# Zero matmuls in TensorE's first gaps, longer planned DMA times, and another order of the first loads in a planned attention-and-mixer kernel

## The chip, the cores and the metric

The kernel runs on one core of a Trainium2 chip. A core has five engines with queues of their own, each working strictly in the order of its queue: TensorE (PE in the profile, its weight loads PEld), VectorE (DVE), ScalarE (ACT), GpSimd (POOL) and SyncE (SP), and DMA engines that all queues share. Loads that change the type from fp32 to fp16 are issued by POOL; transposes by DMA and the stores are issued by SP. The metric is the device time of one execution in microseconds (us), and less is better. Times are medians of several executions; the profile is of one execution.

## The reference

Two stages follow each other. The first is sigmoid attention over 8 batches, 12 heads, 448 positions and 64 values a head; the second is a mixer over the result laid out as 448 x 768:

```
scores = q @ k.T / sqrt(64) - log(448)
attn   = sigmoid(scores) @ v                 # per batch and head
x      = attn laid out as (8, 448, 768)
h      = relu(x.T @ w_tok1) @ w_tok2         # w_tok1 448 x 256, w_tok2 256 x 448
u      = x + h.T
out    = u + relu(u @ w_ch1) @ w_ch2         # w_ch1 768 x 1536, w_ch2 1536 x 768
```

Inputs and output are fp32. The kernel computes in fp16 with fp32 accumulation.

## The kernel before

A batch's attention is cut into three units of four heads, (batch, unit). For each unit k, q and v are loaded, k and q are turned (the 64 head values brought onto the partitions), and seven rounds follow: matmuls of a round's scores (`score`, L499), the sigmoid on ACT (`sig`, L514). After them the value matmuls (`values`, L536) collect the unit's output in PSUM, a copy brings it to SBUF as `xT` (`take`, L567 or L569), and it is turned back into `x`. From a whole `x` follow the token mixing (K1, L721, then relu, then K2, L751, added to x as `u`), a cast and a turn of `u` to `uT`, and the channel mixing: C1 (L828, twelve blocks of six matmuls, relu on DVE) and C2 (L873, and L882 for the tail rows of two batches together).

Batches 0 and 1 are turned by TensorE (`tk` and `tq`, L456, copied from PSUM by DVE at L469). From batch 2 on POOL permutes k and q (`permute`, L433) and SP turns them by DMA (kT, qT, L438); SP also turns `xT` to `x` (L578) and `u` to `uT` (L808), and stores the output. Batch 0's chain is finer: its token mixing runs by unit (K1 at L621, relu, then KT at L650, which adds the second product onto the unit's values in PSUM, and the copy to `uT`, L665 on ACT or L667 on DVE).

Nothing of the order is left to the hardware: every step is an `Op` with an engine, an estimated time, the steps that it follows and the buffers that it uses, and `Plan.run` lays all of them out by a list schedule with these estimates. The outcome is a fixed instruction order for each engine. Where a real time is longer than the estimate, the engine waits at that place and everything behind it waits too. Four estimates matter here. `lag` is what lies between the end of a step and the start of one on another engine. A load's time is a pipe that all loads share (`pipe`), with at most eight DMAs of POOL outstanding (`landed`). A DMA transpose of SP ends at `far`, 3.0 us, after its start, and up to 5 us later while loads are planned to be under way. `choose` picks TensorE's next step by readiness and priority: steps in `extra` by their own `pri` (0 to 2.5 for the turns and batch 0's chain), attention groups by due times, then K, C1 and C2.

Before any data is there, `run_up` (L411) lets TensorE multiply zeros nine times, into a PSUM bank called `idle`. That is one of four banks which the turns, the units' values, K and C all share; `idle` goes back once its users have ended. Loads of POOL come in a written order; from unit 6 on, each load also waits for a sigmoid of the unit three places before it (the `mark` copies, L685).

One thing in the code acts otherwise than it reads: the closures `keep`, `relu` and `lay` of batch 0 read `last` when they are emitted, and by then it holds the value of the last unit. The copy of the second half of `uT` therefore runs on ACT (L665) for all three units, while the plan counts it on DVE for the first two.

Of the kernel before, what the change touches and what calls it, by code (L numbers as in the profile page):

```python
# [55 lines left out]
class Plan:  # L56
# [4 lines left out]
    def __init__(self, pools):  # L61
        self.pools, self.slots, self.ops = pools, {}, []
        self.log, self.kept = [], {}
        self.far = 3.0
        self.landed, self.pipe = [0.0] * 8, 0.0

    def buf(self, *a, **k):
# [2 lines left out]
    def op(self, name, engine, us, emit, after=(), uses=(), rank=0.0):  # L70
        o = Op(name, engine, us, emit, after, uses, rank)
        self.ops.append(o)
        return o

    def lag(self, d, o):
        return 0.0 if d.engine == o.engine == "PE" else self.LAG[d.engine]

    def slot_time(self, held, o):
# [39 lines left out]
    def run(self, choose):  # L118

        lists = {}  # L120
        for o in self.ops:
            if o.engine != "PE":
                lists.setdefault(o.engine, []).append(o)
        free = dict.fromkeys([*lists, "PE", "POOL"], 0.0)
        free["POOL"] = 1.3
        mode = [None]
        left = len(self.ops)
        while left:
            best = None
            for e, ops in lists.items():  # L130
                if e == "LD":
                    ops = ops[:1]
                for o in ops:
                    r = self.ready(o)
                    if r is None:
                        continue
                    at = free[e]
                    if e == "LD":
                        at = max(free["POOL"], self.landed[-8])
                    key = (max(r, at), o.rank, r)  # L140
                    if best is None or key < best[0]:
                        best = (key, e, o)
            pick = choose(self, free["PE"])
            if pick is not None:
                t, ops, kind = pick
                if best is None or t <= best[0][0]:
                    for o in ops:
                        r = self.ready(o)
                        t = max(t, r, free["PE"])
                        if kind != mode[0]:  # L150
                            t += 0.1
                            mode[0] = kind
                        self.hold(o)
                        o.start, o.end = t, t + o.us
                        free["PE"] = t = o.end
                        self.log.append(o)
                        left -= 1
                    continue
            if best is None:
                raise RuntimeError(  # L160
                    "\n".join(
                        f"{o.name} <- {[d.name for d in o.after if d.end is None]}"
                        for o in self.ops
                        if o.start is None
                    )[:6000]
                )
            (t, _, _), e, o = best
            self.hold(o)
            o.start = t
            if e == "LD":  # L170
                free["POOL"] = t + o.n * o.issue
                slow = 1.0 if self.pipe > 8.0 else 1.5
                self.pipe = max(self.pipe, free["POOL"] + 1.5) + slow * o.us
                o.end = self.pipe
                self.landed += [o.end] * o.n
            elif e == "SP":
                free[e] = t + o.us
                o.end = t + self.far + min(5.0, max(0.0, self.pipe - t - 0.5))
            else:
                o.end = free[e] = t + o.us  # L180
            lists[e].remove(o)
            self.log.append(o)
            left -= 1
        self.log.sort(key=lambda o: o.start)
        for o in self.log:
            o.emit()
# [3 lines left out]
def kernel(  # L190
# [12 lines left out]
    nc = tc.nc  # L203
# [7 lines left out]
    NQ = H // 4  # L211
    NDB = D // 128
    NCB = CC // 128
    DH = D // 2
    att_scale = 1.0 / math.sqrt(E)
    att_bias = -math.log(S)
    LEAD, SPAN, REST, WIDE = 12.0, 0.86, 1.0, 2

    assert (B, H, S, E) == (8, 12, 448, 64) and D == 768 and TT == 256 and CC == 1536

# [2 lines left out]
    plan = Plan({"sbuf": pa, "psum": pp})  # L223
# [31 lines left out]
    def mm(n):  # L255
        return n / 2400 + 0.003
# [50 lines left out]
        yield op(f"ld_{what}_{b}_{m}", "LD", 1.12, emit, uses=[t])  # L307

    def load_all(b, m):
        parts = {what: load_qkv(b, m, what) for what in ("k", "q", "v")}  # L310
        if (b, m) == (0, 0):
            for _ in range(2):
                for what in ("k", "q"):
                    o = next(parts[what])
                    loads[(b, m, what)][0].append(o)
        for what, ops in parts.items():
            made = list(ops)
            loads[(b, m, what)][0].extend(made)

    def load_w_tok():  # L320
        view = moe_w_tok1.rearrange("(p j) t -> p j t", j=J)

        def emit():
            nc.gpsimd.dma_start(out=w_tok1[0:64, :, :], in_=view)
            for slot, j0, n in ((0, 4, 3), (3, 3, 1), (4, 0, 3)):
                nc.gpsimd.dma_start(
                    out=w_tok1[64:128, slot : slot + n, :], in_=view[:, j0 : j0 + n, :]
                )

        a = op("ld_tok1", "LD", 2.3, emit, uses=[w_tok1])  # L330
        a.n, a.issue = 4, 0.54

        def emit2():
            nc.gpsimd.dma_start(
                out=w_tok2_s[:, :, :],
                in_=moe_w_tok2.rearrange("(tc t) s -> t tc s", tc=2),
            )
# [3 lines left out]
        for a_, z, j, n in ((0, 6, 0, 3), (1, 6, 4, 3), (6, 8, 3, 1), (8, 14, 4, 3), (9, 14, 0, 3)):  # L341
# [7 lines left out]
            spreads.append(  # L349
                op(f"spread{a_}", "DVE", 0.45, spread, [b], [w_tok2_s, w_tok2], rank=-1 if a_ < 7 else 2)  # L350
            )
        return a, spreads

    def load_ch1(i):
        def emit():
# [17 lines left out]

        return op(f"ld_ch2_{i}", "LD", 3.9, emit, uses=[w_ch2[i]])

    load_all(0, 0)
    load_all(0, 1)
    tok1_ld, tok2_ld = load_w_tok()
    load_all(0, 2)
    ch1_ld, ch2_ld = [], []  # L380
    load_all(1, 0)
    ch1_ld.append(load_ch1(0))
# [32 lines left out]
    up = op("up", "PE", 3.4, run_up, [blank_op], [idle, uT[0]])  # L415
    up.pri = -2
    extra.append(up)

    def turned(b, m, what, side):

# [22 lines left out]
            return [op(f"turn{what}_{b}_{m}", "SP", 1.3, turn, [o], [t, pm], rank=0)] * 2, t  # L443
        parts = [range(2)] if (b, m) != (0, 0) else [range(1), range(1, 2)]
        done = []
        hold = uT_ops[0][-2:] if (b, m) == (1, 2) else []
        for hs in parts:
            ps = bank(f"t{what}_{b}_{m}_{hs[0]}", [128, J, 2, P], FP16)
            r = slice(64 * hs[0], 64 * hs[-1] + 64)
# [26 lines left out]
    def attention(b):  # L476
# [4 lines left out]
        for m in range(NQ):  # L481
# [164 lines left out]
            for s in range(2):  # L646
# [14 lines left out]
                extra.append(o)  # L661

                def keep(s=s, m=m, ps=pa_):
                    if s == 1 and last:
                        nc.scalar.activation(out=uT[0][:, 2 * m + s, :], in_=ps[s](every), func=COPYF)  # L665
                    else:
                        nc.vector.tensor_copy(out=uT[0][:, 2 * m + s, :], in_=ps[s](every))  # L667

                uT_ops[0].append(
                    op(f"uT_{b}_{m}_{s}", "ACT" if s == 1 and last else "DVE", 0.6, keep, [o], [ps[s], uT[0]], rank=-2.5)  # L670
                )
        return rounds

# [23 lines left out]
    def token(b):  # L697
# [12 lines left out]
        else:  # L710
# [3 lines left out]
            for n, c in enumerate(cuts):  # L714
                need = [x_ops[(b, m)][-1 if b < 2 else n] for m in range(NQ)]
                for t in range(2):
# [9 lines left out]
                                stop=(blk == 3),  # L726
                            )

                    o = op(f"K1_{b}_{n}_{t}", "PE", 4 * mm(DH), tok1, [*need, tok1_ld], [ps, X[b], w_tok1, h1[b]])
                    first.append(o)  # L730

                    def relu(ps=ps, c=c, t=t):
# [243 lines left out]
    def choose(plan, t):  # L976
# [14 lines left out]
        for rank, kinds in ((2, K), (3, C1), (4, C2)):  # L991
            n = 0
            for row in kinds:
# [12 lines left out]
                        break  # L1006
                if n > (3 if rank == 2 else 0):
                    break
        if not cands:
            return None  # L1010
        first = min(c[0] for c in cands)
# [37 lines left out]
```

## Time and profile before

| what | value |
|---|---|
| median of 3 runs | 404.08 us (403.29 to 408.87) |
| the profiled execution's own time | 407.89 us |
| its span, first to last instruction | 406.1 us |
| PE busy in it | 375.8 us (93%) |
| ACT, DVE, POOL busy | 206.3, 160.7, 116.2 us |
| mean granted TensorE clock | 0.967 |

The profile shows one execution. Rows of a timeline give the start and duration of a run of instructions in us, the engine, the line of the kernel, the output and input tiles and shapes, how many, and in brackets how long the engine had been idle and what released it. Rows of a table by stretches give, for a window from A to B, its length, then the busy time of PE, PEld, DVE, ACT and POOL, the granted clock (1.00 is full speed, 0.50 half) and what DMA moved. Of a line's rows, the three numbers after a count are the smallest, median and largest duration in ns, and the last two the first and last start. Names such as `x<-xT` say which tile is written from which. SPq is SP's queue, which issues the transposes.

### The profile page before, as it was taken

The page shows a single profiled execution, that of the slowest core. Times are in us where ns is not written, and L with a number is a line of the kernel's source. Part 1 is how long each engine was busy: PE and PEld are TensorE (multiplying, and loading weights), DVE is VectorE, ACT ScalarE, POOL GpSimd, SP SyncE. Part 2 cuts the span into 40 slices and gives each one's busy share as a digit, 9 for nine tenths or more (in the row PEclk, how much of TensorE's full clock was granted, in tenths as well). Part 3 has the DMA queues.
Part 4 walks back from the last instruction along what each step waited for, and adds up shares of the span by engine and source line. Part 5 has one row for each costly group of instructions (what it writes and reads, how often), then busy time and mean ns, then how long its engine had stood idle before and what let it go on. Part 6 is the DMA issues. An engine that isn't in the chain of part 4 may idle for free.

```text
span 406.1 us, 7874 instructions
## 1 busy us (share of the span) xinstructions
PE 375.8 (93%) x3213; PEld 193.2 (48%) x3213; DVE 160.7 (40%) x295; ACT 206.3 (51%) x253; POOL 116.2 (29%) x264
## 2 busy tenths in 40 slices
PE   7889999999979996798999995799999999999995
PEld 3446545545434542354445552344445556555563
DVE  3155545265333422352341341363342245754231
ACT  3686666568746754285646754287564460300000
POOL 9773136333334433224341423223300000000000
PEclk9599999999999999799999999699999999999998
DMA  6999999969996999399958999599902454500343
GB/s 83 171 172 205 209 199 144 151 93 169 118 136 111 183 201 124 50 141 158 147 84 149 159 172 167 78 154 151 135 2 65 105 117 95 109 0 2 77 97 98
DMA packets 98724, 50.56 MB, mean 124 GB/s; under 512 B 72320, under 2 KB 95040, under 8 KB 98688
## 3 DMA queue, kind: packets, MB, share of 16 engines
q0 software_dynamic: 24320, 21.93, 40.9%
q1 hardware_dynamic: 74368, 28.13, 38.2%
q8 instruction: 25, 0.41, 0.4%
q14 instruction: 11, 0.09, 0.1%
HBM read 43.84 MB, written 11.01 MB: 135 GB/s over the span
## 4 chain that ended last, share of the span: by engine, by line
PE 82%; DMA 8%; ACT 5%; POOL 2%; DVE 1%; issue 1%; SPq 0%; POOLq 0%; ACTq 0%
PE c L828 26%; PE c L873 22%; PE qk L499 10%; PE xa L536 8%; PE yn L751 5%; DMA x<-xT 5%; PE k L721 5%; ACT attn L514 3%; PE c L882 3%; DMA uT<-u 2%; DMA k<-in_k_dram 1%; PE tq L456 1%; PE tk L456 1%; ACT u L780 1%; POOL k L291 1%
## 5 line engine op out<-in xcount | busy, mean ns | idle before, releaser
L514 ACT ACTIVATE attn<-qk,att_bias 128x896 f16<-128x896 f32 (+1 forms) x172 | 161.2, 989 | 101.3 <-PE qk L499 101.0
L828 PE MATMUL c<-uT,w_ch 128*128 128x448 f16 x576 | 117.8, 353 | 3.4 <-DMA uT<-u 3.2
L873 PE MATMUL c<-w_ch,h2aT 128*128 128x384 f16 x576 | 98.8, 326 | 0.0
L853 DVE TENSOR_SCALAR h2aT<-c 128x448 f16<-128x448 f32 x96 | 60.0, 625 | 83.1 <-PE c L828 82.9
L828 PEld LDWEIGHTS <-w_ch 128*128 128x128 f16 x576 | 53.2, 98 | 60.9 <-issue 15.9
L873 PEld LDWEIGHTS <-h2aT 128*128 128x128 f16 x576 | 55.1, 98 | 40.6 <-issue 5.1
L897 DVE TENSOR_TENSOR u<-u,c 128x384 f32<-128x384 f32 x48 | 26.6, 554 | 77.2 <-PE c L873 77.2
L499 PE MATMUL qk<-qT,kT 64*64 64x448 f16 x672 | 53.2, 370 | 1.4 <-ACT attn L514 0.9
L536 PE MATMUL xa<-attn,v 64*64 64x448 f16 x672 | 38.2, 360 | 0.5 <-ACT attn L514 0.5
L721 PE MATMUL k<-x,w_tok 128*128 128x384 f16 x112 | 23.0, 361 | 14.9 <-DMA x<-xT 14.9
L685 POOL COPY mark<-attn 1x1 f16<-1x1 f16 x54 | 9.6, 178 | 88.5 <-ACT attn L514 88.5
L433 POOL COPY kp<-k 128x384 f16<-128x384 f16 (+1 forms) x54 | 21.3, 428 | 45.2 <-DMA k<-in_k_dram 45.2
L569 ACT ACTIVATE xT<-xa 128x448 f16<-128x448 f32 x43 | 21.1, 545 | 19.1 <-PE xa L536 18.0
L499 PEld LDWEIGHTS <-kT 64*64 64x64 f16 x672 | 15.2, 107 | 30.6 <-issue 27.5
L772 DVE TENSOR_TENSOR u<-x,yn 128x384 f32<-128x384 f16 x48 | 24.4, 549 | 10.2 <-PE yn L751 10.1
L433 POOL COPY qp<-q 128x384 f16<-128x384 f16 (+1 forms) x54 | 21.3, 432 | 20.0 <-DMA q<-in_q_dram 14.3
L536 PEld LDWEIGHTS <-v 64*64 64x64 f16 x672 | 19.9, 109 | 14.7 <-issue 3.0
L751 PE MATMUL yn<-h,w_tok 128*128 128x384 f16 x128 | 26.3, 328 | 0.0
L733 DVE TENSOR_SCALAR h<-k 128x384 f16<-128x384 f32 x28 | 15.6, 558 | 25.0 <-PE k L721 23.5
L780 ACT ACTIVATE u<-u 128x768 f16<-128x768 f32 x21 | 17.5, 846 | 15.3 <-DVE u L772 15.3
L721 PEld LDWEIGHTS <-w_tok 128*128 128x128 f16 x112 | 11.2, 106 | 26.6 <-DMA x<-xT 11.2
L751 PEld LDWEIGHTS <-w_tok 128*128 128x128 f16 x128 | 10.9, 98 | 12.5 <-issue 6.4
(56 smaller groups left out, 189.3 us busy)
## 6 DMA issues: line engine op xcount, KB each, us to landing
out_dram<-u SPq DMA_DIRECT2D x48, 192.0 KB, 2.9
k<-in_k_dram POOLq DMA_DIRECT2D x21, 224.0 KB, 5.3
q<-in_q_dram POOLq DMA_DIRECT2D x21, 224.0 KB, 4.8
v<-in_v_dram POOLq DMA_DIRECT2D x21, 224.0 KB, 5.2
w_ch<-in_moe_w_ch_dram POOLq DMA_DIRECT2D x6, 768.0 KB, 16.0
out_dram<-ut SPq DMA_DIRECT2D x8, 192.0 KB, 3.1
v<-in_v_dram POOLq DMA_DIRECT2D x6, 112.0 KB, 4.8
x<-xT SPq DMA_TRANSPOSE x36, 4.4
```

The source lines that it names most:

```text
L433: nc.gpsimd.tensor_copy(out=pm[:, to, :, :], in_=src[:, fr, :, :])
L499: nc.tensor.matmul(out=ps[64 * s : 64 * s + 64, h, 0:S], lhsT=kT[64 * h : 64 * h + 64, i, s, :], rhs=qT[64 * h : 64 * h + 64, :, s, :], st ...
L514: nc.scalar.activation(out=at[:, hs, :], in_=ps[:, hs, 0:S], func=SIGMOID, bias=bias_t[:, :], scale=att_scale,)
L536: nc.tensor.matmul(out=ps[s](slice(64 * h, 64 * h + 64)), lhsT=vf[64 * s : 64 * s + 64, h, order[i], :], rhs=attn[i][64 * s : 64 * s + 64, ...
L721: nc.tensor.matmul(out=ps[:, :], lhsT=w_tok1[:, w1_slot(side, blk), 128 * t : 128 * t + 128], rhs=X[b][:, x_block(side, blk), c], start=(b ...
L751: nc.tensor.matmul(out=ps[:, :], lhsT=w_tok2[:, t, s0 : s0 + 2, :], rhs=h1[b][:, t, c], start=(t == 0), stop=(t == 1),)
L772: nc.vector.tensor_tensor(out=to, in0=x, in1=y, op=ADD)
L780: nc.scalar.activation(out=u16[rows, :], in_=utile[rows, :] if blk == 3 else u[b][:, blk, :], func=COPYF)
L828: nc.tensor.matmul(out=to(), lhsT=w_ch1[cb // 4][:, db, 128 * (cb % 4) : 128 * (cb % 4) + 128], rhs=uT[b][:, db, :], start=(db == 0), stop ...
L853: nc.vector.tensor_scalar(out=h2aT[b][:, cb, :], in0=to(), scalar1=0.0, scalar2=None, op0=MAX)
L873: nc.tensor.matmul(out=ps[:, :], lhsT=h2aT[b][:, cb, 128 * blk : 128 * blk + 128], rhs=w, start=(cb == 0), stop=(cb == NCB - 1),)
L897: nc.vector.tensor_tensor(out=t, in0=t, in1=ps[:, :], op=ADD)
```

## The change

Five things differ.

1. Planned times: `far` goes from 3.0 to 4.5 us; a load counts as landed 2.0 us later than the pipe says once the pipe is past 50 us (`load_far`); and 2.0 us instead of 0.12 us are planned between a step of POOL and the step of SP that follows it (`sp_wait`), which are the permutes and the turns of batches 2 to 7.
2. Fillers: while the plan's time is between 4 and 21 us (`FILL`), and no step of TensorE is ready within 0.2 us, the plan puts in one matmul of zeros, 128x128 by 256 columns, counted at 0.11 us. They write the bank `idle`; one last filler, made ahead, is put in at 21 us, and until then the bank is not given back.
3. The first loads: k and q of unit (0,0), k and q of (0,1), v of (0,0), a first part of w_tok1 (three DMAs, what batch 0 needs), w_tok2, k and q of (0,2), v of (0,1), v of (0,2), and the rest of w_tok1 (two DMAs; K1 of odd batches follows it). Before, k, q and v of (0,0) and of (0,1) came first, then all of w_tok1 (four DMAs), w_tok2, then k, q and v of (0,2).
4. The turns of unit (1,1) are held until batch 0's last `uT` copies are done, as those of (1,2) were already.
5. The second half of `uT` is copied by DVE for unit (0,0), and by ACT for (0,1) and (0,2), in the plan and in what is emitted.

```diff
--- before.py
+++ after.py
@@ -61,7 +61,7 @@
     def __init__(self, pools):
         self.pools, self.slots, self.ops = pools, {}, []
         self.log, self.kept = [], {}
-        self.far = 3.0
+        self.far, self.load_far, self.sp_wait = 4.5, 2.0, 2.0
         self.landed, self.pipe = [0.0] * 8, 0.0
 
     def buf(self, *a, **k):
@@ -73,6 +73,8 @@
         return o
 
     def lag(self, d, o):
+        if d.engine == "POOL" and o.engine == "SP":
+            return self.sp_wait
         return 0.0 if d.engine == o.engine == "PE" else self.LAG[d.engine]
 
     def slot_time(self, held, o):
@@ -124,8 +126,8 @@
         free = dict.fromkeys([*lists, "PE", "POOL"], 0.0)
         free["POOL"] = 1.3
         mode = [None]
-        left = len(self.ops)
-        while left:
+        self.left = len(self.ops)
+        while self.left:
             best = None
             for e, ops in lists.items():
                 if e == "LD":
@@ -154,7 +156,7 @@
                         o.start, o.end = t, t + o.us
                         free["PE"] = t = o.end
                         self.log.append(o)
-                        left -= 1
+                        self.left -= 1
                     continue
             if best is None:
                 raise RuntimeError(
@@ -168,10 +170,11 @@
             self.hold(o)
             o.start = t
             if e == "LD":
+                far = self.load_far if self.pipe > 50.0 else 0.0
                 free["POOL"] = t + o.n * o.issue
                 slow = 1.0 if self.pipe > 8.0 else 1.5
                 self.pipe = max(self.pipe, free["POOL"] + 1.5) + slow * o.us
-                o.end = self.pipe
+                o.end = self.pipe + far
                 self.landed += [o.end] * o.n
             elif e == "SP":
                 free[e] = t + o.us
@@ -180,7 +183,7 @@
                 o.end = free[e] = t + o.us
             lists[e].remove(o)
             self.log.append(o)
-            left -= 1
+            self.left -= 1
         self.log.sort(key=lambda o: o.start)
         for o in self.log:
             o.emit()
@@ -215,6 +218,7 @@
     att_scale = 1.0 / math.sqrt(E)
     att_bias = -math.log(S)
     LEAD, SPAN, REST, WIDE = 12.0, 0.86, 1.0, 2
+    FILL = 21.0
 
     assert (B, H, S, E) == (8, 12, 448, 64) and D == 768 and TT == 256 and CC == 1536
 
@@ -307,29 +311,29 @@
         yield op(f"ld_{what}_{b}_{m}", "LD", 1.12, emit, uses=[t])
 
     def load_all(b, m):
-        parts = {what: load_qkv(b, m, what) for what in ("k", "q", "v")}
-        if (b, m) == (0, 0):
-            for _ in range(2):
-                for what in ("k", "q"):
-                    o = next(parts[what])
-                    loads[(b, m, what)][0].append(o)
-        for what, ops in parts.items():
-            made = list(ops)
+        for what in ("k", "q", "v"):
+            made = list(load_qkv(b, m, what))
             loads[(b, m, what)][0].extend(made)
 
-    def load_w_tok():
+    def load_w_tok1(part):
+
         view = moe_w_tok1.rearrange("(p j) t -> p j t", j=J)
+        moves = (
+            ((0, 0, 0, 4), (64, 0, 4, 3), (64, 3, 3, 1)),
+            ((0, 4, 4, 3), (64, 4, 0, 3)),
+        )[part]
 
         def emit():
-            nc.gpsimd.dma_start(out=w_tok1[0:64, :, :], in_=view)
-            for slot, j0, n in ((0, 4, 3), (3, 3, 1), (4, 0, 3)):
+            for r, slot, j0, n in moves:
                 nc.gpsimd.dma_start(
-                    out=w_tok1[64:128, slot : slot + n, :], in_=view[:, j0 : j0 + n, :]
+                    out=w_tok1[r : r + 64, slot : slot + n, :], in_=view[:, j0 : j0 + n, :]
                 )
 
-        a = op("ld_tok1", "LD", 2.3, emit, uses=[w_tok1])
-        a.n, a.issue = 4, 0.54
-
+        a = op(f"ld_tok1_{part}", "LD", 1.3 if part == 0 else 1.0, emit, uses=[w_tok1])
+        a.n, a.issue = len(moves), 0.58
+        return a
+
+    def load_w_tok2():
         def emit2():
             nc.gpsimd.dma_start(
                 out=w_tok2_s[:, :, :],
@@ -349,7 +353,7 @@
             spreads.append(
                 op(f"spread{a_}", "DVE", 0.45, spread, [b], [w_tok2_s, w_tok2], rank=-1 if a_ < 7 else 2)
             )
-        return a, spreads
+        return spreads
 
     def load_ch1(i):
         def emit():
@@ -373,10 +377,25 @@
 
         return op(f"ld_ch2_{i}", "LD", 3.9, emit, uses=[w_ch2[i]])
 
-    load_all(0, 0)
-    load_all(0, 1)
-    tok1_ld, tok2_ld = load_w_tok()
-    load_all(0, 2)
+    early = {(m, what): load_qkv(0, m, what) for m in range(NQ) for what in ("k", "q", "v")}
+
+    def load_early(m, *what):
+        for _ in range(2):
+            for x in what:
+                for o in early[(m, x)]:
+                    loads[(0, m, x)][0].append(o)
+                    if m == 0 and x != "v":
+                        break
+
+    load_early(0, "k", "q")
+    load_early(1, "k", "q")
+    load_early(0, "v")
+    tok1_ld = load_w_tok1(0)
+    tok2_ld = load_w_tok2()
+    load_early(2, "k", "q")
+    load_early(1, "v")
+    load_early(2, "v")
+    tok1_late = load_w_tok1(1)
     ch1_ld, ch2_ld = [], []
     load_all(1, 0)
     ch1_ld.append(load_ch1(0))
@@ -415,6 +434,20 @@
     up = op("up", "PE", 3.4, run_up, [blank_op], [idle, uT[0]])
     up.pri = -2
     extra.append(up)
+    fill = {"n": 0}
+
+    def filler():
+
+
+        def emit():
+            nc.tensor.matmul(
+                out=idle[:, 0:256], lhsT=uT[0][:, 0, 0:128], rhs=uT[0][:, 0, 0:256], start=True, stop=True
+            )
+
+        fill["n"] += 1
+        return op(f"fill_{fill['n']}", "PE", 0.11, emit, [up], [idle])
+
+    fill["last"] = filler()
 
     def turned(b, m, what, side):
 
@@ -443,7 +476,7 @@
             return [op(f"turn{what}_{b}_{m}", "SP", 1.3, turn, [o], [t, pm], rank=0)] * 2, t
         parts = [range(2)] if (b, m) != (0, 0) else [range(1), range(1, 2)]
         done = []
-        hold = uT_ops[0][-2:] if (b, m) == (1, 2) else []
+        hold = uT_ops[0][-2:] if b == 1 and m else []
         for hs in parts:
             ps = bank(f"t{what}_{b}_{m}_{hs[0]}", [128, J, 2, P], FP16)
             r = slice(64 * hs[0], 64 * hs[-1] + 64)
@@ -661,13 +694,13 @@
                 extra.append(o)
 
                 def keep(s=s, m=m, ps=pa_):
-                    if s == 1 and last:
+                    if s == 1 and m:
                         nc.scalar.activation(out=uT[0][:, 2 * m + s, :], in_=ps[s](every), func=COPYF)
                     else:
                         nc.vector.tensor_copy(out=uT[0][:, 2 * m + s, :], in_=ps[s](every))
 
                 uT_ops[0].append(
-                    op(f"uT_{b}_{m}_{s}", "ACT" if s == 1 and last else "DVE", 0.6, keep, [o], [ps[s], uT[0]], rank=-2.5)
+                    op(f"uT_{b}_{m}_{s}", "ACT" if s == 1 and m else "DVE", 0.6, keep, [o], [ps[s], uT[0]], rank=-2.5)
                 )
         return rounds
 
@@ -726,7 +759,7 @@
                                 stop=(blk == 3),
                             )
 
-                    o = op(f"K1_{b}_{n}_{t}", "PE", 4 * mm(DH), tok1, [*need, tok1_ld], [ps, X[b], w_tok1, h1[b]])
+                    o = op(f"K1_{b}_{n}_{t}", "PE", 4 * mm(DH), tok1, [*need, tok1_ld, *([tok1_late] if side else [])], [ps, X[b], w_tok1, h1[b]])
                     first.append(o)
 
                     def relu(ps=ps, c=c, t=t):
@@ -1006,6 +1039,22 @@
                         break
                 if n > (3 if rank == 2 else 0):
                     break
+        if t >= FILL and fill["last"]:
+            extra.append(fill["last"])
+            fill["last"] = None
+        if 4.0 < t < FILL and (not cands or min(c[0] for c in cands) > t + 0.2) and up.start is not None:
+            o = fill.get("op")
+            if o is None or o.start is not None:
+                o = fill["op"] = filler()
+                plan.left += 1
+            state["chosen"] = (t, 0, [o], "128", [o], o)
+            return t, [o], "128"
+        o = fill.get("op")
+        if o is not None and o.start is None:
+            plan.ops.remove(o)
+            idle.users.remove(o)
+            plan.left -= 1
+            fill["op"] = None
         if not cands:
             return None
         first = min(c[0] for c in cands)
```

## The prediction

> **What bounds the kernel now.** I began with the page's busy times, then the waits of TensorE and of SP's queue.
>
> ```profile
> span 406.1 us, 7874 instructions
> PE 375.8 (93%) x3213; PEld 193.2 (48%) x3213; DVE 160.7 (40%) x295; ACT 206.3 (51%) x253; POOL 116.2 (29%) x264
> PEclk9599999999999999799999999699999999999998
> PE k L721 <- DMA x<-xT: 14.9, 5, 6.0
> PE c L828 <- DMA uT<-u: 3.2, 2, 2.2
> SPq L438 <- PE qk L499: 111.7, 13, 51.0
> ```
>
> TensorE bounds it: 375.8 of 406.1 us. What can go is its 30.3 us of idle time and what three half-clock stretches cost (the dips in PEclk: slices 2, 17 and 26, about 10, 161 and 254 us). The two waits for DMA transposes make 18.1 us, all of it after 115 us. The rest lies in the first 45 us and at the two ends.
>
> The stretches tell when the clock falls (columns: PE, PEld, DVE, ACT, POOL busy, granted clock, DMA share, GB/s):
>
> ```profile
> 4.20:7.61 3.41, 2.10 (x27) 1.39 (x25) 1.34 (x3) 0.00 (x0) 3.41 (x7) 1.00 0.85 99
> 7.61:11.03 3.42, 2.37 (x23) 0.95 (x19) 1.14 (x2) 3.22 (x6) 3.42 (x7) 1.00 1.04 141
> 11.03:14.44 3.41, 2.49 (x20) 1.69 (x20) 0.12 (x1) 1.89 (x3) 3.30 (x7) 0.50 1.15 163
> 14.44:17.85 3.41, 3.05 (x26) 1.60 (x28) 1.13 (x2) 1.81 (x4) 1.84 (x4) 0.50 1.17 188
> 17.85:21.27 3.42, 3.42 (x40) 2.13 (x43) 0.00 (x0) 2.55 (x3) 2.43 (x5) 0.50 1.14 168
> 249.96:253.37 3.41, 1.11 (x6) 0.49 (x5) 0.65 (x2) 1.63 (x2) 0.89 (x2) 1.00 1.26 208
> 7.81:35.41 27.60, 23.75 (x281) 13.86 (x280) 10.82 (x22) 22.39 (x29) 20.07 (x31) 0.81 1.15 175
> ```
>
> The clock fell at 11.03, after a stretch with 2.37 of 3.42 us busy, and stayed at half for 10.24 us, until a stretch had been full (3.42 of 3.42). In the head ACT is the nearest bound: batch 0's first sigmoid starts at 7.81, its last ends at 35.41, and ACT worked 22.39 of these 27.60 us. So no more than 5.2 us are to be had there.
>
> The two long stalls, each with what went before it:
>
> ```profile
> 157.92 0.57 PE L499 MATMUL qk<-qT,kT 64*64 64x448 f16 x8
> 164.53 4.49 PE L721 MATMUL k<-x,w_tok 128*128 128x384 f16 x16 [6.04 <-DMA x<-xT]
> 154.14 0.98 ACT L569 ACTIVATE xT<-xa 128x448 f16<-128x448 f32 x2 [2.75 <-PE xa L536]
> 157.45 1.19 POOL L433 COPY qp<-q 128x384 f16<-128x384 f16 x3 [4.85 <-DMA q<-in_q_dram]
> L438 SPq DMA_TRANSPOSE qT<-qp x1: 1222/1222/1222, 158.7 to 158.7; - x1
> L578 SPq DMA_TRANSPOSE x<-xT x2: 1217/1247/1277, 160.0 to 161.3; - x2
> DMA to landing us min/median/max: 4.5/4.6/4.8
> ```
>
> `xT` was complete at 155.12, but its transposes left at 160.0 and 161.3. In front of them SP's fixed order held the turn of q, whose permute ended at 158.64 because q's load was late. The same order stands at the other stall:
>
> ```profile
> 249.76 1.31 PE L828 MATMUL c<-uT,w_ch 128*128 128x448 f16 x6
> 256.44 2.72 PE L721 MATMUL k<-x,w_tok 128*128 128x384 f16 x8 [5.37 <-DMA x<-xT]
> 259.08 0.96 PE L499 MATMUL qk<-qT,kT 64*64 64x448 f16 x8
> 243.46 0.98 ACT L569 ACTIVATE xT<-xa 128x448 f16<-128x448 f32 x2 [2.44 <-PE xa L536]
> L438 SPq DMA_TRANSPOSE qT<-qp x1: 1223/1223/1223, 247.5 to 247.5; - x1
> L578 SPq DMA_TRANSPOSE x<-xT x2: 1216/1666/2117, 250.1 to 252.3; - x2
> DMA to landing us min/median/max: 5.9/6.1/6.3
> 82.11 2.71 PE k L721 x16
> ```
>
> `xT` was ready at 244.44; a turn of q left at 247.5, and x behind it at 250.1. Both stalls cost the clock as well: 16 matmuls of K1 took 4.49 us where they take 2.71 (1.8 more); in the second, eight took 2.72 for half of 2.71, and a score group 0.96 for 0.57 (1.75 more). The last stretch in the table above is this one: 1.11 of 3.41 busy, and the clock fell.
>
> **Part by part: longer planned times.** They change no instruction, only the orders. Set beside the chip's own medians:
>
> ```profile
> k<-in_k_dram POOLq DMA_DIRECT2D x21, 224.0 KB, 5.3
> x<-xT SPq DMA_TRANSPOSE x36, 4.4
> DMA to landing us min/median/max: 2.4/4.4/7.3
> ```
>
> The old plan gave a transpose 3.0 us with no load under way, the new one 4.5, against 4.4 measured. For a load it gave 0.72 to issue, 1.5 to begin and 1.12 to move, 3.3 in all; 2.0 more make 5.3, the measured 5.3. With 1.9 more behind a permute, a turn is planned about 4 us later after its load (`far` moves what lies behind the turn).
>
> Stall at 158.49: the turn left 3.6 us after `xT` was ready (158.7 less 155.12), 4 us move it behind, so x leaves at about 155.2 and 156.4 and lands (4.5, 4.8) at 159.7 and 161.2. TensorE would still be 1.2 and 2.7 early in its old order; planned 1.5 later, K1 waits 1.2 at most. Gain 6.04 - 1.2 + 1.8 = 6.6. At 251.07: x leaves at 244.5 and 245.7, lands by the same 6.1 at 250.6 and 251.8; nothing is left, 5.37 + 1.75 = 7.1. The other five waits are 14.9 + 3.2 - 6.04 - 5.37 = 6.7 together, none over 2.2; 1.5 less of each leaves 0.7: gain 6.0. In all 19.7 of 21.6.
>
> That is the upper end, with the old positions. Six batches have two K1 waits and one for `uT`, 18 waits; a plan at the median leaves about half of them late, by something between 0 and 7.3 - 4.4 = 2.9: nine waits at a quarter of that, 7 us, as an estimate from the spread. And work must be there to put in front; each x and each `uT` is now 1.5 later, and where mixing is short that is idle time. Against that stands the end of the trace:
>
> ```profile
> 350.08 23.84 PE c L828 x126
> ```
>
> 126 matmuls are 21 blocks of C1 in a batch's row of 12, so nine of batch 6 were still waiting, and all of its C2 too. The late batches have cover, the early ones may not; I take 2 us for it. So 19.7 - 7 - 2 = **11 us** gained. Bounds: the whole 19.7; 0 if the stalls only move, and -9 by the third rival below.
>
> **Fillers, load order, turns, copies.** All act before 45 us:
>
> ```profile
> 1.17 3.36 PE L411 MATMUL idle<-uT 128*128 128x448 f16 x9 [1.17 <-DVE uT L404]
> 10.85 1.77 POOL L326 DMA_DIRECT2D w_tok<-in_moe_w_tok_dram  x3
> 11.95 0.93 PE L456 MATMUL tk<-ident,k 128*64 128x128 f16 x7 [1.45 <-DMA k<-in_k_dram]
> 18.09 1.38 PE L536 MATMUL xa<-attn,v 64*64 64x448 f16 x12
> 25.68 0.78 PE L456 MATMUL tq<-ident,q 128*64 128x128 f16 x14
> 29.46 0.54 ACT L665 ACTIVATE uT<-xa 128x448 f16<-128x448 f32 x1
> 44.29 1.31 PE L828 MATMUL c<-uT,w_ch 128*128 128x448 f16 x6
> ```
>
> Zero matmuls do count for the clock: nine of them (3.36 us) were all that had run when the turns began at full clock. How many fillers come: from 4.20 to 21.27 TensorE was idle 17.07 - 13.43 = 3.6 us; of its 8.96 us of work at half clock from 11.03 on, half would go, 4.5 more. So up to 8 us are to fill. Lying in idle time they cost nothing; where a load lands later than planned, what was put in before it is work that the wait no longer absorbs, and I bound this by 1.45, the longest such wait. If the clock holds, 4.5 us of TensorE time go, of which the chain of batch 0 takes no more than ACT's 5.2. The bank `idle`, held to 21, leaves three; the values of (0,0) take two, so turns then follow each other in one.
>
> An issue is 1.77 / 3 = 0.59. k of (0,1) comes two issues earlier, so the wait of 1.45 at 11.95 shrinks by 1.2; q of (0,2) comes three issues (v of (0,1) two, w_tok1 one) and so 1.8 us earlier. v of (0,0) is four later, 2.4 us; its reader starts at 18.09, and a v DMA issued at 8 would have 10 us to land. The one DMA more (0.59) delays batch 1's loads, whose readers wait for batch 0 anyway; the late part of w_tok1 is first read at 82.11.
>
> The turns of (1,1), 2 x 0.78 = 1.6 us, leave a stretch where TensorE waits for DVE and ACT and move into the dense part: about 1 us lost, less 0.3 for a chain that they interrupt. The copy takes 0.54 off ACT; DVE, busy 10.82 of 27.60, has room.
>
> I take 3 of ACT's 5.2 us, since fixed fillers pass lateness on, and 1 off for the turns: C1 begins at 42.3 instead of 44.29, **2 us** gained. The upper bound is 5.2 + 0.5 - 1 = 4.7; the lower is -3, a stretch at half clock (1.7) and the lateness passed on (1.45).
>
> The Trainium skill (TensorE: Matmul & The Clock Gate, Part 1, "HAM oscillation") says that the clock falls after an idle gap of over about 3 us, and by that rule the fillers would save nothing, since the gaps here were at most 1.45 and the head's gain would be the load order's 1.2. The trace speaks against it: the fall at 11.03 came with 2.37 of 3.42 busy. At 161 and 253 the gaps were 6.04 and 5.37, and there it agrees.
>
> **Sum.** 407.89 - 11 - 2 = 394.9 for an execution like the profiled one, which lies 3.8 above the median; with the same offset 391.1. I say 391.
>
> **Rivals.**
>
> *The stalls only move* (22%). Waits are longest where loads and transposes compete, and a list schedule with other costs has other coincidences. Then the head alone counts: 404.08 - 2 = 402. For: the landing spread of 2.4 to 7.3. Against: both long stalls have one cause, which the costs name.
>
> *The clock falls in the head anyway* (11%). In the stretch at 4.20, 21 of 27 matmuls are turns and score matmuls fill a quarter of the array. If fillers were too few, each filler would take double, but a filled stretch raises the clock again, as at 21.27: one stretch, 1.7 us, plus 1.45 of lateness passed on and the 2 not gained: 391 + 5 = 396. The skill has a rule for it (the same page, Part 4): transposes do not count as busy in the same way. No fall came after the stretch of turns at 4.20, so the trace bears it out only in part.
>
> *A turn blocks x by its slot* (12%), the slower end. SP's turns wait 111.7 us for score groups to free `kT`. If mixing is put before score groups, a turn placed ahead of x waits for a group that is itself late. The plan avoids it as long as real and planned times agree within the 2.0 of `sp_wait`; beyond that each unit boundary costs what 158 cost, 6.04 + 1.8 = 7.8. At four boundaries (two of which cost that now): 31 for 21.6, 404 + 9 = 413.
>
> **Numbers.** The forecast has 55%, with 384 to 398 as its own range. A measurement of this kernel tells about 2% from no change: 396.0 and 412.2. Under 396 lie nearly all of the forecast and half of the second rival: 58%. Over 412.2 most of the third: 9%. The rest, 33%, is within. 383 to 405 leaves out the third rival and the far ends.
>
> **What would show it.** Clock: PEclk 1.00 in all stretches from 4.2 to 21, with rows of zero matmuls of 256 columns. Head: C1's first row near 42 instead of 44.29. Orders: x's transposes leaving within 1.5 us of `xT`'s end, no wait of K1 over 3 us, the clock whole after 100 us, and the two DMA waits together near 9 instead of 18.1. The forecast is wrong if these waits stay above 15, or if C1 begins later than 44.

## The result

The changed kernel takes 385.61 us (median of 4, 385.3 to 385.74), the kernel before 403.69 beside it: a ratio of 0.9525, interval 0.9445 to 0.9604, 18.1 us less. The forecast was 391 within 383 to 405. The profiled execution took 385.59 us.

The page of the changed kernel (span, busy times, granted clock in tenths):

```profile
span 383.8 us, 7923 instructions
PE 373.1 (97%) x3240; PEld 193.1 (50%) x3240; DVE 161.0 (42%) x296; ACT 206.8 (54%) x252; POOL 118.6 (31%) x265
PEclk9999999999999999999999999999999999999999
```

TensorE's waits for DMA transposes in it (us in total, times, longest):

```profile
PE k L754 <- DMA x<-xT: 0.4, 1, 0.4
PE c L861 <- DMA uT<-u: 0.3, 1, 0.3
```

The two profiled spans differ by 22.3 us. TensorE's idle time fell from 30.3 to 10.7 us, which is 19.6; of that 17.4 are the two waits, from 18.1 to 0.7. The other 2.7 are busy time: the clock row shows no half clock any more, and 27 zero matmuls more had to run.

The place of the old 6.04 us stall, now at 155 us. In the timeline TensorE, POOL's permute and ACT's copy:

```profile
152.75 2.44 PE L861 MATMUL c<-uT,w_ch 128*128 128x448 f16 x12
155.12 0.57 PE L532 MATMUL qk<-qT,kT 64*64 64x448 f16 x8
155.63 2.77 PE L754 MATMUL k<-x,w_tok 128*128 128x384 f16 x16
146.82 1.19 POOL L466 COPY qp<-q 128x384 f16<-128x384 f16 x3 [1.53 <-DMA q<-in_q_dram]
148.47 0.98 ACT L602 ACTIVATE xT<-xa 128x448 f16<-128x448 f32 x2 [2.75 <-PE xa L569]
```

and the transposes of x, which leave SP's queue from the first to the last start shown:

```profile
L611 SPq DMA_TRANSPOSE x<-xT x2: 1216/1322/1428, 149.7 to 151.2; - x2
```

`xT` ends at 149.45 and x leaves at 149.7: nothing holds it. Here the turn of q still stands ahead of x; its permute ran at 146.82, early enough not to matter. Besides, TensorE has two more blocks of C1 and a score group in front of K1.

That q came early lies in POOL's queue. First the kernel before, then the changed one, around the same load of q:

```profile
149.78 1.19 POOL L433 COPY kp<-k 128x384 f16<-128x384 f16 x3 [4.41 <-DMA k<-in_k_dram]
151.04 0.72 POOL L302 DMA_DIRECT2D q<-in_q_dram  x1
139.95 0.72 POOL L306 DMA_DIRECT2D q<-in_q_dram  x1 [0.28 <-issue]
142.96 1.18 POOL L466 COPY kp<-k 128x384 f16<-128x384 f16 x3 [2.29 <-DMA k<-in_k_dram]
```

Before, the load of q was issued behind the permute of k, which itself waited 4.41 us for its load; now it is issued ahead of that permute. Over the whole trace POOL's permutes waited 59.5 us for loads before and 21.3 now.

At the place of the other stall the order is exchanged. K1 in the timeline:

```profile
234.57 1.46 PE L754 MATMUL k<-x,w_tok 128*128 128x384 f16 x8
236.88 1.47 PE L754 MATMUL k<-x,w_tok 128*128 128x384 f16 x8 [0.35 <-DMA x<-xT]
```

and SP's transposes of x and of q:

```profile
L611 SPq DMA_TRANSPOSE x<-xT x2: 1217/1511/1805, 230.6 to 232.5; - x2
L471 SPq DMA_TRANSPOSE qT<-qp x1: 1248/1248/1248, 233.8 to 233.8; - x1
```

x leaves at 230.6 and 232.5, the turn of q behind it at 233.8; 0.35 us is all that K1 waits.

The stretch from 4.20 to 21.27, in which the clock fell before (busy time of PE, PEld, DVE, ACT, POOL, the clock, DMA):

```profile
4.20:21.27 17.07, 16.70 (x189) 9.79 (x187) 7.38 (x16) 11.79 (x16) 16.18 (x27) 1.00 1.09 156
```

The rest of batch 0's chain in TensorE's timeline:

```profile
38.50 1.16 PE L683 MATMUL xa<-w_tok,h 128*128 128x448 f16 x4 [0.52 <-DVE h L671]
39.49 1.14 PE L784 MATMUL yn<-h,w_tok 128*128 128x384 f16 x6
43.97 2.44 PE L861 MATMUL c<-uT,w_ch 128*128 128x448 f16 x12
```

TensorE is nearly full (16.70 of 17.07 us) and at full clock, and yet C1 begins at 43.97 instead of 44.29. Nearly all of the gain thus comes later.

### The profile page after: what moved, and what is told of

The parts are those of the page before. It is cut to its first block, busy times and chain, and to the rows that moved or that the text cites. A ratio compares the mean times of both kernels' runs of the same rounds, so it can differ in the third digit from the quotient of the medians.

```text
span 383.8 us, 7923 instructions
## 1 busy us (share of the span) xinstructions
PE 373.1 (97%) x3240; PEld 193.1 (50%) x3240; DVE 161.0 (42%) x296; ACT 206.8 (54%) x252; POOL 118.6 (31%) x265
## 4 chain that ended last, share of the span: by engine, by line
PE 87%; DMA 6%; POOL 3%; ACT 2%; DVE 1%; issue 1%; SPq 0%; POOLq 0%; ACTq 0%
PE c L861 29%; PE c L906 24%; PE qk L532 9%; PE xa L569 8%; PE yn L784 5%; PE k L754 5%; PE c L915 3%; DMA k<-in_k_dram 3%; DMA uT<-u 1%; DMA x<-xT 1%; POOL k L295 1%; POOL q L295 1%; PE k L654 1%; ACT attn L547 1%; POOL w_tok L328 1%
## 5 line engine op out<-in xcount | busy, mean ns | idle before, releaser
L532 PE MATMUL qk<-qT,kT 64*64 64x448 f16 x672 | 52.2, 362 | 0.1
L569 PE MATMUL xa<-attn,v 64*64 64x448 f16 x672 | 37.0, 351 | 0.0
L466 POOL COPY kp<-k 128x384 f16<-128x384 f16 (+1 forms) x54 | 21.3, 431 | 14.0 <-DMA k<-in_k_dram 14.0
L569 PEld LDWEIGHTS <-v 64*64 64x64 f16 x672 | 18.7, 107 | 13.5 <-DMA q<-in_q_dram 1.5
L754 PE MATMUL k<-x,w_tok 128*128 128x384 f16 x112 | 20.2, 327 | 0.4 <-DMA x<-xT 0.4
L784 PEld LDWEIGHTS <-w_tok 128*128 128x128 f16 x128 | 11.2, 98 | 11.7 <-issue 4.9
L306 POOL DMA_DIRECT2D k<-in_k_dram x21 | 15.1, 719 | 6.2 <-issue 5.6
```

The costliest lines, as they stand in the source:

```text
L466: nc.gpsimd.tensor_copy(out=pm[:, to, :, :], in_=src[:, fr, :, :])
L532: nc.tensor.matmul(out=ps[64 * s : 64 * s + 64, h, 0:S], lhsT=kT[64 * h : 64 * h + 64, i, s, :], rhs=qT[64 * h : 64 * h + 64, :, s, :], st ...
L569: nc.tensor.matmul(out=ps[s](slice(64 * h, 64 * h + 64)), lhsT=vf[64 * s : 64 * s + 64, h, order[i], :], rhs=attn[i][64 * s : 64 * s + 64, ...
L754: nc.tensor.matmul(out=ps[:, :], lhsT=w_tok1[:, w1_slot(side, blk), 128 * t : 128 * t + 128], rhs=X[b][:, x_block(side, blk), c], start=(b ...
L784: nc.tensor.matmul(out=ps[:, :], lhsT=w_tok2[:, t, s0 : s0 + 2, :], rhs=h1[b][:, t, c], start=(t == 0), stop=(t == 1),)
```

## The experiments

Each kernel ran beside the kernel before, and groups of four shared its runs: 405.5 us for the first group, 407.64 for the second, 406.99 for the third, where medians alone are compared. (In the third group one run of the kernel before took 398.89 us, the other six 406.2 to 410.28.) The three groups ran on different chips, and the kernel before came out up to 4 us apart beside the four sets of runs, so a difference of 1 or 2 us between kernels of different groups is not shown by them.

**Planned times alone.** In the kernel before:

```diff
-        self.far = 3.0
+        self.far = 4.5
     def lag(self, d, o):
+        if d.engine == "POOL" and o.engine == "SP":
+            return 2.0
...
-                o.end = self.pipe
+                o.end = self.pipe + (2.0 if late else 0.0)
```

(`late` is `self.pipe > 50.0` before the load is added.)

> The kernel before with the three planned times alone (far 4.5, load_far 2.0, sp_wait 2.0), nothing else. Theory (planned times make the middle's gain): the two waits for DMA transposes fall from 18.1 us to under 4, the clock stays whole after 100 us, and the time is 14 to 17 us under the kernel before, about 388. Rival (the head makes it: clock and load order): 1 to 5 us under, since the half clock from 11 to 21 us stays.

386.69 us; ratio 0.9525 (0.9444 to 0.9607), 18.8 us less. The page's clock row:

```profile
PEclk9699999999999999999999999999999999999998
```

and the only wait of TensorE for a DMA transpose:

```profile
PE c L831 <- DMA uT<-u: 1.5, 1, 1.5
```

This part has the change's whole gain, to within the interval, although the clock still falls in the head: it was 0.80, 0.50 and 0.70 in the three stretches from 11.03 to 21.27, half clock for about 6.8 us. Even so C1 begins at 42.99, 1 us earlier than in the changed kernel.

**Its two halves.** `far` alone:

```diff
-        self.far = 3.0
+        self.far = 4.5
```

> The kernel before with far 4.5 alone. If TensorE's order is what counts (K1 and C1 planned 1.5 us later), most of the gain of all three comes: 8 us or more under before. If SP's order is what counts (turns ahead of x), the two long stalls stay and only the five short waits go: 3 to 6 us under before, with a wait of over 4 us left.

402.11 us; ratio 0.9875 (0.9793 to 0.9958), 3.4 less, a small gain whose size these runs leave open. The waits for transposes:

```profile
PE c L828 <- DMA uT<-u: 9.3, 2, 6.7
PE k L721 <- DMA x<-xT: 1.3, 3, 0.6
```

K1 hardly waits, but C1 does, 6.7 us at one place. What went before it on ACT and POOL:

```profile
234.02 0.84 ACT L780 ACTIVATE u<-ut 64x768 f16<-64x768 f32 x1 [0.39 <-DVE ut L772]
238.63 1.18 POOL L433 COPY qp<-q 128x384 f16<-128x384 f16 x3 [4.55 <-DMA q<-in_q_dram]
```

and SP's turn of q and transposes of `u`:

```profile
L438 SPq DMA_TRANSPOSE qT<-qp x1: 1222/1222/1222, 239.8 to 239.8; - x1
L808 SPq DMA_TRANSPOSE uT<-u x2: 1209/1351/1493, 233.7 to 241.2; - x2
```

The last part of `u` was ready at 234.86 and left at 241.2, behind a turn of q whose permute waited for its load: the same cause with another victim. Then `load_far` with `sp_wait`, `far` left at 3.0:

```diff
     def lag(self, d, o):
+        if d.engine == "POOL" and o.engine == "SP":
+            return 2.0
...
-                o.end = self.pipe
+                o.end = self.pipe + (2.0 if late else 0.0)
```

> The kernel before with load_far and sp_wait alone, far still 3.0. If SP's order is what counts: the two long stalls go, 8 to 13 us under before, short waits of 1 to 2 us stay. If TensorE's order counts: under 4 us gained.

391.9 us; ratio 0.9683 (0.9608 to 0.9758), 13.6 less.

```profile
PE c L831 <- DMA uT<-u: 2.4, 1, 2.4
PE k L724 <- DMA x<-xT: 2.3, 3, 1.3
```

Long stalls are gone, short ones stay, as expected of SP's order. This pair of times also gives POOL's queue its new order: the permutes waited 23.2 us for loads, against 59.5 before, 64.5 with `far` alone and 70.0 with `sp_wait` alone (below), so it is `load_far` that does it. `far` on top of it is worth another 5.2 (391.9 to 386.69, timed in one group).

**The order of SP's queue by itself.** The kernel before with all its orders but for two turns:

```diff
         self.log.sort(key=lambda o: o.start)
+        for turn, x in (("turnq_4_2", "x_3_2_1"), ("turnq_6_2", "x_5_2_1")):
+            o = next(o for o in self.log if o.name == turn)
+            self.log.remove(o)
+            self.log.insert([o.name for o in self.log].index(x) + 1, o)
```

> The kernel before with its orders kept, but for two places in SP's order: the turn of q of (4,2) and that of (6,2) go behind the transposes of x that they stood in front of. By the prediction's own terms: the stall of 6.04 shrinks to 1.2 for its first half and no more than 2.7 for all, that of 5.37 to under 1, and the clock does not fall at 161 and 253: 9 to 12 us under before. If these stalls come from the transposes' own time and contention, not from their place in the queue: under 3 us gained.

394.52 us; ratio 0.969 (0.9611 to 0.9768), 11.0 less. TensorE's timeline at the two places:

```profile
158.50 0.57 PE L503 MATMUL qk<-qT,kT 64*64 64x448 f16 x8
159.15 2.77 PE L725 MATMUL k<-x,w_tok 128*128 128x384 f16 x16
244.51 1.46 PE L725 MATMUL k<-x,w_tok 128*128 128x384 f16 x8
```

x's transposes at the first of them:

```profile
L582 SPq DMA_TRANSPOSE x<-xT x2: 1189/1202/1216, 155.3 to 156.6; - x2
```

and all its waits for transposes:

```profile
PE c L832 <- DMA uT<-u: 4.4, 3, 2.1
PE k L725 <- DMA x<-xT: 3.6, 3, 1.5
```

Two instructions of one queue, each moved behind two others, are worth 11 us: x leaves at 155.3, K1 starts 0.08 us after the score group and at full clock. So the transposes' own time and contention did not make the long stalls; 4.4 and 3.6 us of short waits remain.

**`sp_wait` alone.**

```diff
     def lag(self, d, o):
+        if d.engine == "POOL" and o.engine == "SP":
+            return 2.0
```

> The kernel before with sp_wait 2.0 alone. The two turns left 3.6 and 3.1 us after x was ready, so by the prediction's step 1.9 us do not move them behind x: the long stalls stay, less than 4 us gained. If any larger lag between permute and turn does it: 9 us or more.

393.64 us against 406.99: 13.4 less, against my expectation.

```profile
157.09 2.78 PE L723 MATMUL k<-x,w_tok 128*128 128x384 f16 x16 [0.97 <-DMA x<-xT]
242.66 2.20 PE L723 MATMUL k<-x,w_tok 128*128 128x384 f16 x8 [3.34 <-DMA x<-xT]
```

and x's transposes and the turn of q at the first place:

```profile
L580 SPq DMA_TRANSPOSE x<-xT x2: 1190/1213/1236, 152.3 to 153.6; - x2
L440 SPq DMA_TRANSPOSE qT<-qp x1: 1220/1220/1220, 155.3 to 155.3; - x1
```

The first long stall is gone: its turn is behind x in this kernel's order. The second is shorter but there, with its turn still ahead (it left at 235.8, x at 237.2). So how late the chip was (3.6 us) does not tell how far a planned time has to move: the order turns over by the margin within the plan, and 1.9 us were enough for it at one place. The gain is as large as the 13.6 of `load_far` and `sp_wait` together in the first group, so what `load_far` adds in time is not shown, although it changes POOL's waits.

**The rest of the change without the planned times.**

```diff
-        self.far, self.load_far, self.sp_wait = 4.5, 2.0, 2.0
+        self.far, self.load_far, self.sp_wait = 3.0, 0.0, 0.12
```

> The changed kernel with the old planned times (far 3.0, no load_far, sp_wait 0.12); fillers, load order, held turns and copies stay. Theory (the gain in the middle comes from planned times that agree with the chip): 2 to 5 us under before, about 401, with over 10 us of waits for DMA transposes. Rival (any other order loses the two coincidences): 385 to 393, waits under 6 us.

408.39 us; ratio 1.0027 (0.9985 to 1.0069): nothing.

```profile
PE c L861 <- DMA uT<-u: 8.2, 2, 7.1
PE k L754 <- DMA x<-xT: 7.1, 2, 4.6
```

SP's turn of q and the last part of `u` at the longest of them:

```profile
246.23 2.31 SPq L471 DMA_TRANSPOSE qT<-qp  x1
248.63 1.21 SPq L841 DMA_TRANSPOSE uT<-u  x1
```

Another order with the same old times has nearly as much waiting, 15.3 us, and the two long waits stand at the same two turns of q: K1 waits 4.6 us at 159, where x left 2.0 us after `xT` was ready, behind the turn again, and C1 waits 7.1 us at 252, where the last part of `u`, ready at 240.91, left at 248.6 behind the other turn. So not any new order loses the stalls. Nor does the head alone gain anything here: TensorE was busy 16.82 of the 17.07 us from 4.20 to 21.27 at full clock, and C1 began at 44.57, against 44.29 before.

**The head, part by part.** The changed kernel without fillers:

```diff
-    FILL = 21.0
+    FILL = 4.0
-        if 4.0 < t < FILL and (not cands
+        if 4.0 < t < 0.0 and (not cands
```

> The changed kernel without fillers. By the prediction's terms the clock falls at about 11 us and the head loses some 2 us: 387 to 389, C1 beginning about 2 us later than 43.97. Rival (the head is bound by loads and ACT, half a clock costs TensorE nothing that counts): 385 to 386.5, C1 within 0.7 us of 43.97.

(The last filler alone stays, at 4 us, and gives the bank back there.) 384.11 us (383.51 to 384.83); ratio 0.9416 (0.9363 to 0.9468). Two stretches:

```profile
7.61:11.03 3.42, 3.05 (x33) 1.59 (x33) 1.14 (x2) 3.10 (x5) 3.42 (x7) 1.00 1.00 136
11.03:14.44 3.41, 2.63 (x31) 1.53 (x30) 1.25 (x2) 2.79 (x5) 3.11 (x6) 1.00 1.17 182
```

and TensorE's timeline:

```profile
17.68 0.75 PE L489 MATMUL tk<-ident,k 128*64 128x128 f16 x14 [0.23 <-DMA k<-in_k_dram]
21.55 1.03 PE L654 MATMUL k<-x,w_tok 128*128 128x256 f16 x8 [0.24 <-ACT x L636]
42.14 2.06 PE L861 MATMUL c<-uT,w_ch 128*128 128x448 f16 x10
```

Neither expectation held. The clock does not fall without fillers either (the mean was 0.999 to 1.0 in all four executions), and C1 begins 1.8 us earlier. Its median is 1.5 us under the changed one's, but they were not timed in one group.

With the old order of the first loads in the changed kernel, and then without fillers as well:

```diff
-    load_early(0, "k", "q")
-    load_early(1, "k", "q")
-    load_early(0, "v")
-    tok1_ld = load_w_tok1(0)
...
+    load_all(0, 0)
+    load_all(0, 1)
+    tok1_ld, tok2_ld = load_w_tok()
+    load_all(0, 2)
```

> The changed kernel with the old order of the first loads. By the prediction's terms: k of (0,1) comes 1.2 us later and q of (0,2) 1.8 us later, C1 begins 1 to 2 us later, 386.5 to 388. If ACT alone bounds the head: no change, within 0.7 us of 385.6.

384.48 us (383.56 to 385.42); ratio 0.9424 (0.9379 to 0.9469); C1 begins at 43.91. With fillers there, the load order is worth nothing that shows. And beside the kernel without fillers, timed in the same group, the 1.8 us at C1's begin (43.91 against 42.14) are not seen in the medians: 384.48 against 384.11, with ranges that overlap.

> The changed kernel without fillers and with the old order of the first loads (planned times, held turns and copies stay). Theory: fillers and load order each keep the clock by themselves, without both it falls near 11 us as before, and since ACT and the loads bound the head this costs little: 385 to 387. If the half clock costs what the prediction said (2 us and more of the head): 387 to 390.

387.13 us. Its four executions point to a price of the clock: 383.81 us with a mean granted clock of 1.0, and 387.62, 387.17 and 387.08 with 0.985, 0.983 and 0.984, which is 3.3 to 3.8 us more. But only the first has a trace (C1 begins at 42.13 in it, as without fillers alone), so where the clock fell in the others is not seen. With the planned times alone the same comparison gave less: 385.47 us at 0.998, 385.84 at 0.988 and 387.55 at 0.984. A lower clock came in three of four executions where neither fillers nor the new load order are there, and in none of the four without fillers alone. That the load order always prevents it can't be said: in the two further kernels without fillers, below, the mean was 0.989 to 0.999. With fillers and the new planned times it was 0.997 or more in every execution of three kernels.

Then with the bank held but a single filler:

```diff
-        if 4.0 < t < FILL and (not cands
+        if 4.0 < t < 0.0 and (not cands
```

> The changed kernel with one filler only, the last one at 21 us, so that the bank stays held until then but no filler takes TensorE's time. If the held bank is what fillers cost: about 385.6, C1 begins near 43.9. If the fillers' own time in TensorE's fixed order is: about 384.1, C1 near 42.1, as without fillers and with the bank free.

385.87 us (384.74 to 388.26): the median is the one expected of the held bank, but the fastest run lies 0.6 above the other expectation, and the two kernels that it is held against were timed in other groups. C1 begins later than either expectation said. The trace shows the turns one behind the other:

```profile
19.52 0.75 PE L489 MATMUL tk<-ident,k 128*64 128x128 f16 x14 [1.86 <-DMA k<-in_k_dram]
21.50 1.01 PE L622 MATMUL xb<-ident,xT 128*128 128x128 f16 x8 [0.73 <-DVE kT L502]
25.28 1.86 PE L654 MATMUL k<-x,w_tok 128*128 128x256 f16 x8
45.35 2.44 PE L861 MATMUL c<-uT,w_ch 128*128 128x448 f16 x12
```

From tk to K1 lie 5.8 us, without the held bank 3.9 (17.68 to 21.55): xb waits for the copy of kT out of the one bank. But a load was also 1.86 late in this execution and the clock fell after it, so the whole of the 45.35 is not the bank's, and how much it is stays open.

**Held turns.** The changed kernel with the turns of (1,1) free:

```diff
-        hold = uT_ops[0][-2:] if b == 1 and m else []
+        hold = uT_ops[0][-2:] if (b, m) == (1, 2) else []
```

> The changed kernel without the hold on the turns of (1,1). By the prediction's terms: these 1.6 us of turns lie in TensorE's waits again and 0.7 to 1 us are gained, about 384.8. Rival (they break into batch 0's chain by more than they fill): 386 to 387.

387.45 us; ratio 0.9493 (0.9448 to 0.9538), 1.8 above the changed kernel's median where I expected 0.8 below, though in another group, and 3.0 above the kernel with fillers and the old load order of its own group.

```profile
PE c L861 <- DMA uT<-u: 2.6, 2, 2.0
```

C1 begins at 44.44, 0.5 later. The rest is 2.6 us of waits for `uT` in later batches, which may be this order's coincidence; the run does not separate the two.

**Still longer transposes.** Without fillers, and with

```diff
-        self.far, self.load_far, self.sp_wait = 4.5, 2.0, 2.0
+        self.far, self.load_far, self.sp_wait = 5.0, 2.0, 2.0
```

> The changed kernel without fillers and with far 5.0. If 4.5 is already past what the chip needs: within 1 us of the same kernel at 4.5 (384.1), waits for transposes stay near zero. If margin over the median still pays: 0.5 to 1 us less. If longer planned times run out of mixing work: 1 to 4 us more, with idle time before C1 of early batches.

384.76 us, against 384.11 at 4.5: no difference that counts. No wait for a transpose is left, 4.5 is enough, and half a microsecond more does not run out of mixing work: C1 begins at 41.80.

## Why the prediction was right, and where it was not

The size came out between the forecast and its upper end: 13 us were forecast, 18.1 measured. That the sum lies nearer to the result than its larger part does is luck: the planned times gave 7.8 more than their 11, and the head's 2, which did not come, made up for some of it.

*What bounds the kernel, and why the long stalls.* Right. Moving two turns of q behind x gave 11.0 us where 9 to 12 followed from the prediction's terms, clock included. Why q's load was late the prediction did not ask: in POOL's queue it stood behind a permute that waited.

*The planned times, 19.7 - 7 - 2 = 11.* The 19.7 were right (18.8 measured by themselves); the two deductions were mis-sized. "Nine waits at a quarter" of the landing spread were to leave about 9 us of waiting: 0.7 stayed, 1.5 in the kernel with these times alone. The spread was unchanged (2.4, 4.1 and 7.4 us for x's transposes, against 2.4, 4.4 and 7.3), so I take it that late landings met a TensorE that still had other steps in front, by the margin that its own order gives; no run tested this by itself. The 2 us for mixing work that runs out were not needed either; at `far` 5.0 nothing ran out.

*Which of the times does it.* The step by which a turn moves behind x if it is planned later by more than the 3.6 us it was late failed twice. With `sp_wait` alone 1.9 us were enough at that very place. And in the changed kernel the turn there did not move behind x, for all its 4 us: the stall of 6.04 went with q's load issued ahead of k's permute, which by the runs of the two halves is the work of `load_far`, and with more of TensorE's steps in front of K1; no run separates these two. The prediction knew `load_far` as a later time for the turn and gave POOL's order no term.

*The head, 2 us.* The gain was 0.3 at C1's begin (43.97, just inside the 44 that was to prove the forecast wrong) and none that shows in the whole: without the planned times the head's parts gave 1.0027, and with them they added nothing to the 0.9525 that the planned times have alone. Of its terms, the chain did get shorter by about the 2 us named (KT begins at 38.50; the row of before is below), but the held turns and more of K2 (six matmuls at 39.49) stood before C1 then. "Fillers cost nothing in idle time" failed: without them C1 began at 42.14, near the 42.3 of the forecast, though the medians of one group do not show these 1.8 us. The bank that they hold, which the prediction named and gave no price, is the likely reason; the run with the bank alone points to it without settling it. "If the clock holds" was right, and with fillers and the new times it always held, but the load order alone held it mostly too. The price of the fall, 4.5 us of TensorE time of which 3 were to count, stays open: 3.3 to 3.8 us between executions of one kernel, 0.4 and 2.1 between those of another, where C1 began at 42.99 after a fall. The turns' 1 us came out with the other sign, C1 0.5 later without the hold, in one execution.

The row of the kernel before's timeline for it:

```profile
40.56 0.93 PE L650 MATMUL xa<-w_tok,h 128*128 128x448 f16 x4
```

*The rivals.* That the stalls only move is nearer to what happens with the old planned times (15.3 us, at the same two turns, once with C1 as the victim), not with the new. The clock did not fall in the head. Nor does the busy time of a stretch alone say when it falls: 3.05, 2.63 and 2.50 us (the last without fillers and with the old load order) kept it up, and before it fell after 2.37 but not after the 2.10 ahead of that. The Trainium skill's rule of idle gaps (TensorE: Matmul & The Clock Gate, Part 1), which would have kept it up before as well, does not cover this fall. No turn blocked x by its slot: K1 waited 0.4 us in all.

## What to carry to other kernels

Where orders are planned ahead, set the planned time of a transfer to what the trace measures from issue to landing, the steps that feed it included: a too early estimate puts a step that is not ready ahead of ready ones in a strict queue, and one place of this kind can cost 5 to 8 us. Look in the trace for an issue that leaves long after its data were ready, and at what stands in front of it; then at the queue that feeds that one, as POOL's did here. A filler's price is also the buffer that it holds.

## What the runs showed of the hardware

A lower clock was not a property of a program alone: the same kernel kept it at 1.0 in one execution and had a mean of 0.983 to 0.985 in three, 3.3 to 3.8 us apart. And the clock row says 1.00 before the first change is recorded, while the matmuls were slow. The zero matmuls of the kernel before against C1's, same shape (ns: smallest, median, largest):

```profile
L411 PE MATMUL idle<-uT x9: 397/581/581, 1.2 to 4.1; 128*128 128x448 f16 x9
L828 PE MATMUL c<-uT,w_ch x576: 349/352/363, 44.3 to 373.6; 128*128 128x448 f16 x192
```

581 ns against 352 under the same 1.00.
